# The second layer of the last 24 tiles in seven products instead of eight, and q and k turned by DMA

## The chip, the cores and the metric

The kernel runs on one core of a Trainium2 chip. The metric is the device time of one execution in microseconds (us); lower is better. The core has five engines that run side by side and wait for one another by semaphores: PE (TensorE, matmuls; PEld is its loading of weights), DVE (VectorE), ACT (ScalarE), POOL (GpSimd) and SP (SyncE, which here only issues DMAs). Each engine takes its instructions in the order in which they were written.

## The reference

Block-local attention, then a two-layer network on its output. Cut to what matters:

```python
# q, k, v: (8, 8, 576, 64) fp32: batch, heads, tokens, d; nine chunks of 64 tokens
scores = scale * np.matmul(q_c, k_c.transpose(0, 1, 2, 4, 3))   # within a chunk, 64 x 64
scores = scores - np.max(scores, axis=-1, keepdims=True)
attn = np.exp(scores)
attn = attn / (np.sum(attn, axis=-1, keepdims=True) + 1e-09)
out = np.matmul(attn, v_c)
x = out.transpose(0, 2, 1, 3).reshape(4608, 512)
h = x @ w_in                      # 512 x 2048
g = np.maximum(0.01 * h, h)
return g @ w_out                  # 2048 x 512, fp32 result
```

## The kernel before, in words

All matmuls are in fp16 with fp32 sums. The 4608 tokens are 36 tiles (units) of 128 tokens, two chunks of 64 each. The program is one straight list: for every unit an attention round, and between the stages of a round pieces of the two layers for tokens whose attention is done.

**A round** `it` of the main loop (lines 455 to 488) does, in this order: scores of unit it-1 on PE (`stage_s`, Sp, L308, eight matmuls of 64 columns), their maximum and subtraction on DVE (`stage_m`, mx, L317; `stage_b`, sh, L321), exp on ACT (`stage_x`, ex, L327), sums, reciprocal and product on DVE (`stage_z`, z, ze, zi, L333 to L337; `stage_n`, en, L342), the turned probabilities et, for units from 9 on by a DMA transpose that SP issues (`stage_d`, L361), and for unit it-3 the values (`stage_v`, xp, L372) and their copy by ACT into xT (`stage_a`, L385). `fill(n)` between the stages takes n pieces of the layers from a fixed list; 2 + 2 + 2 in rounds to 16, then 2 + 2 + 3.

**q and k.** Scores need q and k with d on the partitions. Units to 8 load whole rows (`load_qk`) and turn them on PE (qp, kp). From unit 9 on, `load_qk_batch` (L86) loads q_d and k_d by 16 DMAs a batch in an order in which DVE's 32x32 block transposes complete the turn: `stage_dq` (L290) twice a round into QZ, which holds q between zeros so that two heads share a matmul, and `stage_dk` (L298) once into KT. These loads, v and the weights are issued by POOL, which casts fp32 to fp16 on the way.

**The layers.** A block is 128, 256 or 512 tokens. First layer (`mm1`, L155): weights w_inT stationary, the block's xT moving, four matmuls a 128-row slice of d_ff; ACT writes the leaky result to gT (`act1`, L170). Second layer (`mm2`, L180): gT stationary, w_outT moving, 16 matmuls of 512 columns a tile of 128 tokens; ACT copies oP to osb (`store`, L191) and SP stores it (L193). One piece is four matmuls of 512 columns or as many columns in narrower ones. The list holds block after block: all of a block's first layer, then all of its second. The last tile is cut in three parts of columns (`last`, L206, L216, L214, L217) so that the last store is small. The start is a list written out by hand (FRONT).

PSUM has four buffers for hT and oP, one each for qp, kp, Sp, and one for tpe and xp.

Of the kernel before, what the change touches and what calls it, by code (L numbers as in the profile page):

```python
# [16 lines left out]
def kernel(  # L17
# [27 lines left out]
    BLOCKS = [128] * 6 + [256] + [128] * 2 + [256] * 5 + [512] * 4  # L45
# [10 lines left out]
    xT = sbp.tile([128, NT, n_tok], FP16, name="xT")  # L56
# [17 lines left out]

    qkd: dict[int, tuple[bass.AP, bass.AP]] = {}

    def load_qk_batch(b):
        both = []
        for name, src in (("q_d", q), ("k_d", k)):
            t = sbp.tile([128, 2, 2, S // 32, 32], FP16, name=name, tag=name, bufs=2)  # L80
            for m in range(2):
                for s in range(2):
                    for dh in range(2):
                        p0 = s * 64 + dh * 32
                        h0 = 4 * m + 2 * s
                        nc.gpsimd.dma_start(  # L86
                            out=t[p0:p0 + 32, m, :, :, :].rearrange("p h b d -> p (h b) d"),
                            in_=src[b, h0:h0 + 2, :, dh * 32:dh * 32 + 32].rearrange("h (b t) d -> t (h b) d", t=32),
                        )
            both.append(t.rearrange("p m h b d -> p (m h) (b d)"))  # L90
        qkd[b] = tuple(both)
# [28 lines left out]
    for eng, name, src in ((nc.sync, "q_f", q), (nc.scalar, "k_f", k)):  # L120
        t = sbp.tile([128, H, D], FP32, name=name)
        eng.dma_start(out=t, in_=src[0, :, 0:G, :].rearrange("h p d -> p h d"))
        first.append(t)
# [8 lines left out]
        "g1 v0 g2 Q0 Q1 g3 Q2 Q3 g4 P0 P1 P2 P3 g5 v1 g6 g7 g8 D2 "  # L132
    )
    LOADERS = {"g": load_qk, "v": load_v, "Q": load_w_in_quarter, "P": load_w_out_quarter, "D": load_qk_batch}
# [6 lines left out]
    gT: dict[int, bass.AP] = {}  # L141
    oP: dict[tuple[int, int], bass.AP] = {}
    START = [sum(BLOCKS[:j]) for j in range(len(BLOCKS))]

    HT: dict[tuple[int, int], bass.AP] = {}
    parts: dict[tuple[int, int], int] = {}

    def mm1(j, a):
        tb, r0 = BLOCKS[j], START[j]
        nf = 512 // tb  # L150
        hT = psp.tile([128, nf, tb], FP32, name="hT", tag="mm", bufs=4)
        for i in range(nf):
            fc = nf * a + i
            for t in range(NT):
                nc.tensor.matmul(  # L155
                    out=hT[:, i, :],
                    lhsT=w_inT[:, t, fc * 128:(fc + 1) * 128],
                    rhs=xT[:, t, r0:r0 + tb],
                    start=(t == 0),
                    stop=(t == NT - 1),  # L160
                )
        HT[j, a] = hT

    def act1(j, a):
        tb = BLOCKS[j]
        nf = 512 // tb
        if j not in gT:
            tag, bufs, pad = ("gS", 4, 128) if tb == 128 else ("gT", 2, 512)
            gT[j] = sbp.tile([128, NFC, tb], FP16, name="gT", tag=tag, bufs=bufs, padded_shape=[128, NFC, pad])
        nc.scalar.activation(  # L170
            out=gT[j][:, nf * a:nf * a + nf, :], in_=HT.pop((j, a)), func=AFT.Prelu, bias=0.0, scale=1.0, alpha=0.01
        )

    def mm2(j, ti, part):
        n = parts.get((j, ti), 0)
        if n == 0:
            oP[j, ti] = psp.tile([128, d_model], FP32, name="oP", tag="mm", bufs=4)
        o = oP[j, ti]
        for fc in range(part * 4, part * 4 + 4):
            nc.tensor.matmul(  # L180
                out=o,
                lhsT=gT[j][:, fc, ti * 128:(ti + 1) * 128],
                rhs=w_outT[:, fc, :],
                start=(n == 0 and fc == part * 4),
                stop=(n == NFC // 4 - 1 and fc == part * 4 + 3),
            )
        parts[j, ti] = n + 1

    def store(j, ti):
        osb = sbp.tile([128, d_model], FP32, name="osb", tag="osb", bufs=3)  # L190
        nc.scalar.activation(out=osb, in_=oP.pop((j, ti)), func=AFT.Copy, bias=0.0, scale=1.0)  # L191
        r0 = START[j] + ti * 128
        nc.sync.dma_start(out=out[r0:r0 + 128, :], in_=osb)  # L193

    def last(j, ti):
        r0 = START[j] + ti * 128
        osb = sbp.tile([128, d_model], FP32, name="osb", tag="osb", bufs=3)
        for c0, c1, copy, queue in (
            (0, d_model // 2, nc.scalar, nc.sync),
            (d_model // 2, 3 * d_model // 4, nc.scalar, nc.scalar),  # L200
            (3 * d_model // 4, d_model, nc.vector, nc.sync),
        ):
            part = slice(c0, c1)
            o = psp.tile([128, d_model], FP32, name="oP", tag="mm", bufs=4)
            for fc in range(NFC):
                nc.tensor.matmul(  # L206
                    out=o[:, :c1 - c0],
                    lhsT=gT[j][:, fc, ti * 128:(ti + 1) * 128],
                    rhs=w_outT[:, fc, part],
                    start=(fc == 0),  # L210
                    stop=(fc == NFC - 1),
                )
            if copy is nc.vector:
                copy.tensor_copy(out=osb[:, part], in_=o[:, :c1 - c0])  # L214
            else:
                copy.activation(out=osb[:, part], in_=o[:, :c1 - c0], func=AFT.Copy, bias=0.0, scale=1.0)  # L216
            queue.dma_start(out=out[r0:r0 + 128, part], in_=osb[:, part])  # L217

    def c1(j):
        return [("mm1", j, a, 0) for a in range(NFC * BLOCKS[j] // 512)]  # L220
# [3 lines left out]

    chunks = []
    for j in range(len(BLOCKS)):
        chunks += c1(j) + c2(j)
    state = {"tokens": 0}

    def fill(n):  # L230
        for _ in range(n):
            if not chunks:
                return
            kind, j, a, p = chunks[0]
            if START[j] + BLOCKS[j] > state["tokens"]:
                return
            chunks.pop(0)
            if kind == "mm1":
                mm1(j, a)
                act1(j, a)  # L240
            elif j == len(BLOCKS) - 1 and a == BLOCKS[j] // 128 - 1:
                if p == 0:
                    last(j, a)
# [4 lines left out]

# [29 lines left out]
    def stage_k(u):  # L278
        KT[u] = sbp.tile([128, 4, 2, CH], FP16, name="KT", tag="KT", bufs=3)
        nc.scalar.activation(out=KT[u], in_=KP.pop(u), func=AFT.Copy, bias=0.0, scale=1.0)  # L280

    def cuts(u):
        r0, r1 = u * G, (u + 1) * G
        cut = min(-(-r0 // S) * S, r1) if r0 % S else r1
        return [(a // S, a % S, (a - r0) // CH, (z - a) // CH) for a, z in ((r0, cut), (cut, r1)) if a < z]

    def stage_dq(u, s):
        qz = QZ[u % NQZ]
        for b, at, e0, n in cuts(u):
            nc.vector.transpose(  # L290
                out=qz[s * CH:(s + 1) * CH, :, e0:e0 + n, s, :],
                in_=qkd[b][0][s * CH:(s + 1) * CH, :, at:at + n * CH].rearrange("p h (e t) -> p h e t", e=n),
            )

    def stage_dk(u):
        KT[u] = sbp.tile([128, 4, 2, CH], FP16, name="KT", tag="KT", bufs=3)
        for b, at, e0, n in cuts(u):
            nc.vector.transpose(  # L298
                out=KT[u][:, :, e0:e0 + n, :],
                in_=qkd[b][1][:, :, at:at + n * CH].rearrange("p h (e t) -> p h e t", e=n),  # L300
            )

    def stage_s(u):
# [7 lines left out]
        SP[u] = Sp  # L311

    MX: dict[int, bass.AP] = {}

    def stage_m(u):
        MX[u] = sbp.tile([128, 8], FP32, name="mx", tag="mx", bufs=2)
        nc.vector.tensor_reduce(out=MX[u], in_=SP[u], axis=AXL.X, op=ALU.max)  # L317

    def stage_b(u):
# [3 lines left out]
        )  # L323

    def stage_x(u):
        E[u] = sbp.tile([128, 8, CH], FP16, name="ex", tag="ex", bufs=2)
        nc.scalar.activation(out=E[u], in_=SH.pop(u), func=AFT.Exp, bias=0.0, scale=SCL)  # L327

    ZI: dict[int, bass.AP] = {}

    def stage_z(u):
# [5 lines left out]
        nc.vector.reciprocal(out=ZI[u], in_=ze)  # L337

    def stage_n(u):
# [4 lines left out]
        )  # L344

    def stage_e(u):
# [4 lines left out]
        TP[u] = tpe  # L351

    def stage_c(u):
# [3 lines left out]
        ET[u] = et  # L357

    def stage_d(u):
# [4 lines left out]
        ET[u] = et  # L364

    def stage_v(u):
        et = ET.pop(u)
        xp = psp.tile([128, NT, 2, CH], FP32, name="xp", tag="ox", bufs=1)
        for e in range(2):
            b, c = divmod(2 * u + e, NCH)  # L370
            for t in range(NT):
# [3 lines left out]
                    rhs=et[:, t // 2, e, t % 2, :] if u < UD else et[:, t % 2, e, t // 2, :],  # L375
# [3 lines left out]
            if c == NCH - 1 and b + NVB < B:  # L379
                load_v(b + NVB)  # L380
        XP[u] = xp

    def stage_a(u):
        xp = XP.pop(u)
        nc.scalar.activation(out=xT[:, :, u * G:(u + 1) * G], in_=xp, func=AFT.Copy, bias=0.0, scale=1.0)  # L385
        state["tokens"] = (u + 1) * G


    def idle(n):
        t = psp.tile([128, 4, 128], FP32, name="idle", tag="mm", bufs=4)  # L390
# [3 lines left out]
    def first_layer(j, a):  # L394
        chunks.remove(("mm1", j, a, 0))
        mm1(j, a)

    def second_layer(j, p):
        chunks.remove(("mm2", j, 0, p))
        mm2(j, 0, p)  # L400
# [53 lines left out]

    for it in range(6, NU + 3):
        dve = UD <= it < NU
# [4 lines left out]
        if dve:  # L461
            stage_dq(it, 0)
# [6 lines left out]
        if dve:  # L469
            stage_dq(it, 1)  # L470
            stage_dk(it)
        elif it < UD:
# [4 lines left out]
            stage_k(it)  # L477
        if it <= NU:
# [41 lines left out]
```

## Time and profile before

| What | Value |
|---|---|
| median of 3 runs | 294.21 us (294.01 to 294.56) |
| profiled execution, span from first to last instruction | 292.1 us (no other time of it is given) |
| PE busy | 283.5 us, 2564 matmuls |
| DVE busy | 183.8 us, 343 instructions |
| ACT busy | 155.2 us, 268 instructions |
| POOL busy | 119.5 us, 148 instructions |
| hT, L155, 1152 matmuls | 135.1 us |
| oP, L180, 560 matmuls | 128.6 us |
| QZ, L290, 60 transposes | 38.2 us |
| KT, L298, 30 transposes | 19.4 us |

The busy time of an engine is the union of its instructions. A group's mean is the length of one instruction with its latency, so for pipelined matmuls it is longer than the distance from one start to the next. A wait line names who waited, for whom, the total, the number of times and the longest. A timeline line gives start, length, engine, line, operation, output <- inputs, count, and in brackets the idle time before it with what ended it.

### The profile page before, as it was taken

The page shows a single profiled execution, that of the slowest core. Times are in us where ns is not written, and L with a number is a line of the kernel's source. Part 1 is how long each engine was busy: PE and PEld are TensorE (multiplying, and loading weights), DVE is VectorE, ACT ScalarE, POOL GpSimd, SP SyncE. Part 2 cuts the span into 40 slices and gives each one's busy share as a digit, 9 for nine tenths or more (in the row PEclk, how much of TensorE's full clock was granted, in tenths as well). Part 3 has the DMA queues.
Part 4 walks back from the last instruction along what each step waited for, and adds up shares of the span by engine and source line. Part 5 has one row for each costly group of instructions (what it writes and reads, how often), then busy time and mean ns, then how long its engine had stood idle before and what let it go on. Part 6 is the DMA issues. An engine that isn't in the chain of part 4 may idle for free.

```text
span 292.1 us, 6233 instructions
## 1 busy us (share of the span) xinstructions
PE 283.5 (97%) x2564; PEld 181.0 (62%) x2564; DVE 183.8 (63%) x343; ACT 155.2 (53%) x268; POOL 119.5 (41%) x148
## 2 busy tenths in 40 slices
PE   4989999999999999999999999999999999999995
PEld 4979845888677766767676744444445444444444
DVE  6987417789899998777787788778876730000000
ACT  6457623666555555646564647734873377127511
POOL 8867547998408936913295369130000000000000
PEclk9999999999999999999999999999999999999999
DMA  9999999999969999999499399999111320120022
GB/s 132 169 193 193 203 157 198 151 148 144 124 97 96 162 78 158 154 142 90 101 107 132 61 159 147 78 65 163 54 20 54 73 91 0 38 81 28 0 74 72
DMA packets 192476, 32.00 MB, mean 110 GB/s; under 512 B 183488, under 2 KB 187968, under 8 KB 192448
## 3 DMA queue, kind: packets, MB, share of 16 engines
q0 software_dynamic: 170208, 18.10, 117.7%
q1 hardware_dynamic: 21056, 13.18, 18.1%
q10 hardware_dynamic: 1184, 0.33, 0.5%
q8 instruction: 20, 0.33, 0.5%
q14 instruction: 8, 0.07, 0.1%
HBM read 36.70 MB, written 9.44 MB: 158 GB/s over the span
## 4 chain that ended last, share of the span: by engine, by line
PE 93%; DVE 3%; DMA 2%; ACT 1%; issue 1%; DVEq 0%
PE hT L155 43%; PE oP L180 41%; PE xp L372 3%; PE Sp L308 3%; DMA k_f<-in_k_dram 2%; PE oP L206 1%; PE tpe L350 1%; PE kp L268 1%; DVE mx L317 0%; DVE z L333 0%; DVE sh L321 0%; DVE en L342 0%; PE qp L263 0%; ACT ex L327 0%; DVE VB L420 0%
## 5 line engine op out<-in xcount | busy, mean ns | idle before, releaser
L155 PE MATMUL hT<-xT,w_inT 128*128 128x128 f16 (+2 forms) x1152 | 135.1, 272 | 0.2 <-issue 0.2
L180 PE MATMUL oP<-w_outT,gT 128*128 128x512 f16 x560 | 128.6, 379 | 0.0
L155 PEld LDWEIGHTS <-w_inT 128*128 128x128 f16 x1152 | 90.0, 98 | 33.4 <-issue 0.5
L170 ACT ACTIVATE gT<-hT 128x512 f16<-128x512 f32 x144 | 85.7, 596 | 34.8 <-PE hT L155 33.0
L180 PEld LDWEIGHTS <-gT 128*128 128x128 f16 x560 | 52.5, 98 | 55.8
L191 ACT ACTIVATE osb<-oP 128x512 f32<-128x512 f32 x35 | 20.9, 597 | 61.3 <-PE oP L180 58.7
L86 POOL DMA_DIRECT2D q_d<-in_q_dram x48 | 38.7, 821 | 32.0 <-DVE QZ L290 28.0
L317 DVE TENSOR_REDUCE mx<-Sp 128x8 f32<-128x512 f32 x36 | 24.9, 691 | 32.6 <-PE Sp L308 32.5
L86 POOL DMA_DIRECT2D k_d<-in_k_dram x48 | 38.7, 824 | 0.9 <-issue 0.5
L290 DVE STREAM_TRANSPOSE QZ<-q_d 64x512 f16<-64x512 f16 (+1 forms) x60 | 38.2, 644 | 0.4
L214 DVE COPY osb<-oP 128x128 f32<-128x128 f32 x1 | 0.3, 290 | 51.4 <-PE oP L206 51.4
L327 ACT ACTIVATE ex<-sh 128x512 f16<-128x512 f32 x36 | 22.5, 626 | 15.0 <-DVE sh L321 14.8
L385 ACT ACTIVATE xT<-xp 128x512 f16<-128x512 f32 x36 | 21.4, 594 | 16.4 <-PE xp L372 16.3
L95 POOL DMA_DIRECT2D VB<-in_v_dram x16 | 18.5, 1162 | 28.0 <-PE xp L372 28.0
L333 DVE TENSOR_REDUCE z<-ex 128x8 f32<-128x512 f16 x36 | 23.6, 654 | 3.9 <-ACT ex L327 3.8
L342 DVE TENSOR_TENSOR en<-ex,zi 128x512 f16<-128x512 f16 x36 | 24.9, 691 | 1.4 <-DVE zi L337 0.2
L321 DVE TENSOR_TENSOR sh<-Sp,mx 128x512 f32<-128x512 f32 x36 | 24.9, 691 | 1.2
L298 DVE STREAM_TRANSPOSE KT<-k_d 128x512 f16<-128x512 f16 (+1 forms) x30 | 19.4, 654 | 0.8
L372 PEld LDWEIGHTS <-VB 128*128 128x128 f16 x288 | 13.1, 98 | 6.8 <-issue 1.2
L308 PEld LDWEIGHTS <-QZ 128*128 128x128 f16 x288 | 13.2, 99 | 5.4 <-issue 0.3
L372 PE MATMUL xp<-et,VB 128*128 128x64 f16 x288 | 14.3, 193 | 1.1 <-DVE et L356 1.1
L308 PE MATMUL Sp<-KT,QZ 128*128 128x64 f16 x288 | 14.5, 194 | 0.2 <-ACT KT L280 0.2
(37 smaller groups left out, 112.2 us busy)
## 6 DMA issues: line engine op xcount, KB each, us to landing
out_dram<-osb SPq DMA_DIRECT2D x35, 256.0 KB, 2.3
VB<-in_v_dram POOLq DMA_DIRECT2D x16, 288.0 KB, 6.5
q_d<-in_q_dram POOLq DMA_DIRECT2D x48, 72.0 KB, 5.3
k_d<-in_k_dram POOLq DMA_DIRECT2D x48, 72.0 KB, 5.2
w_inT<-in_moe_w_in_dram POOLq DMA_DIRECT2D x8, 256.0 KB, 8.8
w_outT<-in_moe_w_out_dram POOLq DMA_DIRECT2D x4, 512.0 KB, 9.5
q_in<-in_q_dram POOLq DMA_DIRECT2D x7, 128.0 KB, 9.3
k_in<-in_k_dram POOLq DMA_DIRECT2D x7, 128.0 KB, 9.3
```

The costliest lines, as they stand in the source:

```text
L86: nc.gpsimd.dma_start(out=t[p0:p0 + 32, m, :, :, :].rearrange("p h b d -> p (h b) d"), in_=src[b, h0:h0 + 2, :, dh * 32:dh * 32 + 32].rear ...
L155: nc.tensor.matmul(out=hT[:, i, :], lhsT=w_inT[:, t, fc * 128:(fc + 1) * 128], rhs=xT[:, t, r0:r0 + tb], start=(t == 0), stop=(t == NT - 1),)
L170: nc.scalar.activation(out=gT[j][:, nf * a:nf * a + nf, :], in_=HT.pop((j, a)), func=AFT.Prelu, bias=0.0, scale=1.0, alpha=0.01)
L180: nc.tensor.matmul(out=o, lhsT=gT[j][:, fc, ti * 128:(ti + 1) * 128], rhs=w_outT[:, fc, :], start=(n == 0 and fc == part * 4), stop=(n == ...
L290: nc.vector.transpose(out=qz[s * CH:(s + 1) * CH, :, e0:e0 + n, s, :], in_=qkd[b][0][s * CH:(s + 1) * CH, :, at:at + n * CH].rearrange("p ...
L308: nc.tensor.matmul(out=Sp[:, i, :], lhsT=qz[:, 2 * m + g, e, :, :], rhs=kt[:, 2 * m + g, e, :], start=True, stop=True)
L317: nc.vector.tensor_reduce(out=MX[u], in_=SP[u], axis=AXL.X, op=ALU.max)
L321: nc.vector.tensor_tensor(out=SH[u], in0=SP.pop(u), in1=MX.pop(u).unsqueeze(2).to_broadcast((128, 8, CH)), op=ALU.subtract)
L327: nc.scalar.activation(out=E[u], in_=SH.pop(u), func=AFT.Exp, bias=0.0, scale=SCL)
L333: nc.vector.tensor_reduce(out=z, in_=E[u], axis=AXL.X, op=ALU.add)
L342: nc.vector.tensor_tensor(out=E[u], in0=ex, in1=ZI.pop(u).unsqueeze(2).to_broadcast((128, 8, CH)), op=ALU.mult)
L372: nc.tensor.matmul(out=xp[:, t, e, :], lhsT=VB[b % NVB][:, t, c, :], rhs=et[:, t // 2, e, t % 2, :] if u < UD else et[:, t % 2, e, t // 2, :],
```

## The change

**Seven products.** The last 24 tiles become six blocks of 512 tokens. The second layer of such a block, a 512 x 2048 matrix g times w_out (2048 x 512), is cut into 2 x 2 quarters on both sides, and Strassen's scheme forms the four quarters of the result from seven products m1 to m7 of sums of quarters instead of eight products of quarters. Five sums of quarters of w_out (WF) are made once by DVE, in rounds 11 to 15; five sums of quarters of gT (S1, S2, S5, S6, S7) by DVE for each block. Each product is 2 x 8 matmuls of 256 columns into one of three PSUM banks (a, b, c: the buffers of qp and kp and one of the four of hT and oP). m4 adds onto m2's bank, m5 onto m3's, m6 onto m1's, m7 onto m4's. ACT copies out m3, m4, m5 (td, osb), DVE combines the rest (td, tw, tt, osb), and each half of a block, 256 tokens, is stored by one DMA of 512 KB. The last tile's narrow parts are gone.

**q and k.** `load_qk` for all units, six rounds ahead; from unit 9 on, two DMA transposes on SP (`stage_t`, two rounds ahead, in front of et's) turn q and k into QT and KT, and POOL copies QT between the zeros of QZ in two copies of 64x512 (`stage_p`). DVE's block transposes are gone. The next load of v is issued by POOL at the end of a round instead of in its middle.

**Order.** Blocks before the 24 tiles are 6 x 128 and 3 x 256. Products of a block are merged with the first layer of the next one. While the program is built, times are kept for PE, DVE and ACT (T), and `fill` takes the first piece of each kind whose inputs are ready by these times, else the one that is ready earliest. Pieces a round: 6, in rounds 12 to 19 five.

```diff
-    BLOCKS = [128] * 6 + [256] + [128] * 2 + [256] * 5 + [512] * 4
+    BLOCKS = [128] * 6 + [256] * 3 + [512] * 6
+    PLAIN = 9
+    SUB = {7: 128}
+    RING = 1536
+    HB, HM = NFC // 2, d_model // 2
...
+    def weight_form(i):
+        of, by, op = WFORMS[i]
+        nc.vector.tensor_tensor(out=WF[:, i], in0=of, in1=by, op=op)
+        on("dve", 1.24)
...
+        a11, a12 = g[:, :HB, :n], g[:, HB:, :n]
+        a21, a22 = g[:, :HB, n:2 * n], g[:, HB:, n:2 * n]
+        of, by, op, to = {
+            "S2": (a21, a22, ALU.add, None),
+            "S1": (a11, a22, ALU.add, None),
+            "S5": (a11, a12, ALU.add, None),
+            "S6": (a21, a11, ALU.subtract, a21),
+            "S7": (a12, a22, ALU.subtract, a12),
+        }[name]
...
+        nc.vector.tensor_tensor(out=to, in0=of, in1=by, op=op)
+    FORMS = ("S2", "S1", "S5", "S6", "S7")
...
+        for fc in range(HB):
+            nc.tensor.matmul(
+                out=BANK[bank][:, p, :],
+                lhsT=lhs[:, fc, p * 128:(p + 1) * 128],
+                rhs=rhs[:, fc, :],
+                start=(opens and p == 0 and fc == 0),
+                stop=(fc == HB - 1),
...
+        if m == 2:
+            nc.vector.tensor_tensor(out=TMP["d"], in0=TMP["d"], in1=BANK["b"], op=ALU.subtract)
+        elif m == 1:
+            nc.vector.tensor_tensor(out=temp("w", j), in0=BANK["c"], in1=TMP["d"], op=ALU.add)
+        elif m == 5:
+            nc.vector.tensor_tensor(out=temp("t", j), in0=TMP["w"], in1=osb_of(j, 0)[:, :, HM:], op=ALU.subtract)
+        elif m == 6:
+            nc.vector.tensor_tensor(out=osb_of(j, 1)[:, :, HM:], in0=BANK["c"], in1=TMP["d"], op=ALU.add)
+            store_side(j, 1)
+        elif m == 7:
+            nc.vector.tensor_tensor(out=osb_of(j, 0)[:, :, :HM], in0=BANK["b"], in1=TMP["t"], op=ALU.add)
+            store_side(j, 0)
...
+    ORDER = (3, 2, 1, 4, 5, 6, 7)
...
-    def stage_dq(u, s):
-        qz = QZ[u % NQZ]
-        for b, at, e0, n in cuts(u):
-            nc.vector.transpose(
...
+    def stage_t(u):
+        for i, (name, to) in enumerate((("QT", QT), ("KT", KT))):
+            to[u] = sbp.tile([128, 4, 2, CH], FP16, name=name, tag=name, bufs=(3, 6)[i])
+            nc.sync.dma_start_transpose(
+                out=to[u].rearrange("p i e t -> p i (e t)"), in_=qk[u][i].rearrange("p h d -> p (h d)")
+            )
+    def stage_p(u):
+        qt = QT.pop(u)
+        for s in range(2):
+            part = slice(s * CH, (s + 1) * CH)
+            nc.gpsimd.tensor_copy(out=QZ[u % NQZ][part, :, :, s, :], in_=qt[part])
...
+    ROUND = [0] * 6 + [6] * 6 + [5] * 8 + [6] * 8 + [6] * 11
     for it in range(6, NU + 3):
-        dve = UD <= it < NU
         if it <= NU:
             stage_s(it - 1)
             stage_m(it - 1)
             stage_b(it - 1)
-        if dve:
-            stage_dq(it, 0)
         fill(2)
...
+        if UD <= it < NU:
+            stage_p(it)
+        if UD <= it + 2 < NU:
+            stage_t(it + 2)
...
+        if 11 <= it < 16:
+            weight_form(it - 11)
         if it <= NU:
             stage_z(it - 1)
             stage_n(it - 1)
             if it - 1 >= UD:
                 stage_d(it - 1)
         fill(2)
+        due = free_v[:]
         values(it - 2 if it - 2 < UD else it - 3 if it - 3 >= UD else -1)
-        fill(3 if dve and it >= 17 else 2)
-        for b in range(3, B):
-            if it == 9 * b // 2 - 4:
-                load_qk_batch(b)
+        fill(ROUND[it] - 4)
+        for b in due:
+            load_v(b)
+            free_v.remove(b)
+        if UD + 3 <= it + 6 < NU:
+            load_qk(it + 6)
```

More of the change, by code (lines that the diff above doesn't have):

```diff
@@ L186, in mm2 @@
             )
+        on("pe", UNIT)
         parts[j, ti] = n + 1
     def store(j, ti):
-        osb = sbp.tile([128, d_model], FP32, name="osb", tag="osb", bufs=3)
+        osb = sbp.tile([128, d_model], FP32, name="osb", tag="osb", bufs=3, padded_shape=[128, 2 * d_model])
         nc.scalar.activation(out=osb, in_=oP.pop((j, ti)), func=AFT.Copy, bias=0.0, scale=1.0)
+        on("act", 0.62, T["pe"] + 0.2)
         r0 = START[j] + ti * 128
         nc.sync.dma_start(out=out[r0:r0 + 128, :], in_=osb)
[L195 to L217, printed above, removed]
@@ L225, with after, forms @@
     chunks = []
-    for j in range(len(BLOCKS)):
+    for j in range(PLAIN):
         chunks += c1(j) + c2(j)
+    chunks = [x for j in range(PLAIN) for x in c1(j) + c2(j)] + c1(PLAIN)
+    for j in range(PLAIN, len(BLOCKS)):
+        chunks += merged(c7(j), c1(j + 1), 1.5) if j + 1 < len(BLOCKS) else c7(j)
     state = {"tokens": 0}
+    later: list[list] = []
+    def after(n, what):
+        later.append([n, what])
+    sums: list[tuple[int, str]] = []
+    def forms(n, slack=1.0):
+        while n and sums and T["dve"] <= T["pe"] + slack:
+            j, name = sums[0]
+            if when["gT", j] > T["pe"] + slack:
+                return
+            if name in ("S2", "S1", "S5") and j > PLAIN and (j - 1, int(name[1])) not in done:
+                return
+            sums.pop(0)
+            form(j, name)
+            n -= 1
@@ new lines, with ready @@
+    LEFT: dict[int, int] = {}
+    for x in chunks:
+        LEFT[x[1]] = LEFT.get(x[1], 0) + 1
+    def ready(x):
+        kind, j, a, p = x
+        if kind == "mm1":
+            end = START[j] + (p + 1) * sub(j)
+            if end > state["tokens"] or any(LEFT[i] for i in range(j) if tile_of(i) == tile_of(j) - 2):
+                return None
+            return when["x", end]
+        if made.get(j, 0) < NFC * BLOCKS[j] // 512:
+            return None
+        if kind == "mm2":
+            return when["gT", j]
+        needs = [("gT", j), BANKS[a] + (j if a > 3 else j - 1,)]
+        if a not in (3, 4):
+            needs.append((f"S{a}", j))
+        at = 0.0
+        for y in needs:
+            t = when.get(y, 0.0 if y[-1] < PLAIN else None)
+            if t is None:
+                return None
+            at = max(at, t)
+        return at
@@ new lines, with pick @@
+    BANKS = {3: ("evict", 5), 2: ("combine", 7), 1: ("combine", 6), 4: ("combine", 2), 5: ("evict", 3), 6: ("combine", 1), 7: ("evict", 4)}
+    def pick():
+        first: dict[str, tuple] = {}
+        for x in chunks:
+            first.setdefault(x[0], x)
+        can = [(ready(x), x) for x in chunks if first[x[0]] == x]
+        can = [(t, x) for t, x in can if t is not None]
+        if not can:
+            return None
+        if any(0 < n < NFC // 4 for n in parts.values()):
+            can = [(t, x) for t, x in can if x[0] == "mm2"]
+        return next((x for t, x in can if t <= T["pe"]), min(can, key=lambda y: y[0])[1])
@@ L230, in fill, with follow @@
+    def follow():
+        for y in later:
+            y[0] -= 1
+        while any(y[0] < 0 for y in later):
+            y = next(y for y in later if y[0] < 0)
+            later.remove(y)
+            y[1]()
     def fill(n):
         for _ in range(n):
-            if not chunks:
+            x = pick()
+            while x is None and (later or sums):
+                if later:
+                    later.pop(0)[1]()
+                else:
+                    form(*sums.pop(0))
+                x = pick()
+            if x is None:
@@ L233, in fill @@
                 return
[L234 to L237, printed above, removed]
+            T["pe"] = max(T["pe"], ready(x))
+            chunks.remove(x)
+            kind, j, a, p = x
+            LEFT[j] -= 1
             if kind == "mm1":
[L239 to L243, printed above, removed]
+                mm1(j, a, p)
+                act1(j, a, p)
+                if j >= PLAIN and made[j] == NFC * BLOCKS[j] // 512:
+                    sums.extend((j, name) for name in FORMS)
+            elif kind == "m":
+                product(j, a, p)
+                if p == BLOCKS[j] // 256 - 1:
+                    evict(j, a)
+                    if a in (1, 2, 5, 6, 7):
+                        after(1, lambda j=j, a=a: combine(j, a))
@@ L247, in fill @@
                     store(j, a)
+            follow()
+            forms(1)
+            if not chunks:
+                while later:
+                    later.pop(0)[1]()
     QP: dict[int, bass.AP] = {}
```

218 lines of the change are left out of this document (160 added, 58 removed).

## The prediction

> **What bounds the kernel now.** I read the busy shares and the slices first, then what PE waited for, then one stretch of PE and of DVE instruction by instruction, then the groups, the DMAs and the end.
>
> ```profile
> span 292.1 us, 6233 instructions
> PE 283.5 (97%) x2564; PEld 181.0 (62%) x2564; DVE 183.8 (63%) x343; ACT 155.2 (53%) x268; POOL 119.5 (41%) x148
> PE   4989999999999999999999999999999999999995
> ...
> PEclk9999999999999999999999999999999999999999
> ```
>
> PE is full in every slice but the first, the third and the last, at full granted clock. The waits of PE alone:
>
> ```profile
> PE idle L392 <- POOL ident masks.py:199: 3.8, 1, 3.8
> PE xp L372 <- DVE et L356: 1.1, 1, 1.1
> PE hT L155 <- issue: 0.2, 1, 0.2
> PE Sp L308 <- ACT KT L280: 0.2, 1, 0.2
> ```
>
> 5.3 us in all, all in the start. So the time is PE's work plus the two ends, and a PE matmul removed is time removed as long as PE stays fed. What a matmul costs is read from start to start, because ends are modelled (start, length, engine, line):
>
> ```profile
> 121.74 3.62 PE L180 MATMUL oP<-w_outT,gT 128*128 128x512 f16 x16
> 125.19 0.40 PE L372 MATMUL xp<-et,VB 128*128 128x64 f16 x8
> 125.43 2.75 PE L180 MATMUL oP<-w_outT,gT 128*128 128x512 f16 x12
> 128.02 0.40 PE L308 MATMUL Sp<-KT,QZ 128*128 128x64 f16 x8
> 128.25 3.66 PE L155 MATMUL hT<-xT,w_inT 128*128 128x256 f16 x32
> 131.74 0.40 PE L372 MATMUL xp<-et,VB 128*128 128x64 f16 x8
> ```
>
> 512 columns take (125.19-121.74)/16 = 216 ns, 256 columns (131.74-128.25)/32 = 109 ns, eight of 64 columns 0.23 us. Half the columns cost half, new weights each time. A piece of work (four of 512, or eight of 256) is 0.86 to 0.87 us. From 121.51, the Sp before these lines, to the Sp at 128.02 a round of one attention unit takes 6.51 us: seven pieces and 0.46.
>
> **PE's part.** Second layer of the last 24 tiles: now 23 x 16 x 216 ns = 79.4, plus the last tile's narrow parts (line 206, 3.55 us on the chain) = 83.0 us. After: 6 blocks x 7 products x 2 x 8 = 672 matmuls of 256 columns x 109 ns = 73.3. In the first layer 256 matmuls of 256 columns (27.9) become 128 of 512 (27.6). PE loses 9.7 + 0.3 = **10.0 us**. Everything else below is what is given back.
>
> **DVE's part.** Rounds get shorter: 6 pieces and 0.46 = 5.7 us, in rounds 12 to 19 five pieces, 4.8 us. Rows for DVE:
>
> ```profile
> 129.18 0.69 DVE L321 TENSOR_TENSOR sh<-Sp,mx 128x512 f32<-128x512 f32 x1
> 129.78 1.42 DVE L290 STREAM_TRANSPOSE QZ<-q_d 64x512 f16<-64x512 f16 x2
> 131.23 0.71 DVE L298 STREAM_TRANSPOSE KT<-k_d 128x512 f16<-128x512 f16 x1
> 131.87 0.64 DVE L333 TENSOR_REDUCE z<-ex 128x8 f32<-128x512 f16 x1
> ...
> 132.99 0.69 DVE L342 TENSOR_TENSOR en<-ex,zi 128x512 f16<-128x512 f16 x1
> ```
>
> Removed: the three transposes, 2.1 us a round, 57.6 in all (groups of lines 290 and 298). They stood in the shadow of ACT's ex (0.62 us, some 0.85 with its signals). What stays is mx to the end of sh, 1.42, and z to the end of en, 1.81: 3.23 a round.
> Added: 35 sums of 128x2048 16-bit elements (five for the weights, five for each block) and 30 combinations of 128x512 fp32, like sh, 0.69. No row shows a sum of 2048. The fixed part of a DVE instruction comes from QZ's transposes, 701 ns for 512 elements and 416 for 256: 131 ns. The copy et (16-bit in and out) takes 424 ns for 512, so 0.57 ns an element and **1.30 us** for 2048; en (one fp32 operand) takes 691, which makes 2.37. I take 1.30, the row whose operands are all 16-bit, and keep 2.37 as an end. [...]
>
> A block of products fills five rounds (14 pieces and the next block's 16): 28.4 us of PE. DVE there: 5 x 3.23 + 5 x 1.30 + 5 x 0.69 = 26.1, plus ex's shadow where the order of the built kernel puts nothing into it (two rounds of 0.85) or only a combination (two of 0.15): **28.1 of 28.4**. DVE is as full as PE in these 15 rounds. In the second round of a block m2's combination (td) comes after S5, the softmax and en, some 6.0 us into the round, and m4 takes its bank at 6.6: 0.6 us of room. I put 1.0 us for lateness there, between nothing and the rival below. The weight sums stand in ex's shadow in rounds 11 to 15: 1.42 + 1.30 + 1.81 = 4.5 of 4.8, so nothing; uncovered they would cost 6.5.
>
> Two places have no first-layer work to put between products. (a) Block 9, the first: S2 needs ACT's last gT piece and 1.30 us, 2.15 after that piece's matmuls (0.2 signal, 0.60 evict, 1.30, signals), while PE has 1.97 of work; S1 stands behind mx and sh, done at 4.95, where mb ends at 4.0. **1.3 us**. (b) Block 14, the last: S2 0.5 late as ma takes 1.75; then td stands behind S1, S5 and S6 and ends at 6.75, so m4 waits from 5.75 to 6.85. **1.6 us**.
>
> **The end.** Now the last piece is small:
>
> ```profile
> 288.94 0.29 DVE L214 COPY osb<-oP 128x128 f32<-128x128 f32 x1 [51.36 <-PE oP L206]
> 289.26 0.33 SPq L217 DMA_DIRECT2D out_dram<-osb  x1
> ```
>
> From this copy's start to landing 1.9 us (landing 1.6 for 64 KB). After: a combination, 0.69, and a store of 512 KB. Landings in the quiet end are 1.6, 1.7, 2.0 us for 64, 128, 256 KB; doubling once more gives 2.6 (3.5 by the busy median of 2.3). 0.69 + 0.1 + 2.6 = 3.4 to 4.3: **1.6 us** more, at most 2.4.
>
> **SP, POOL, DMA.** SP gets two transposes of q and k a round beside et's, ahead of en's wait:
>
> ```profile
> L361 SPq DMA_TRANSPOSE et<-en x27: 1189/1196/2182, 74.6 to 237.7; - x27
> DMA to landing us min/median/max: 2.4/4.4/6.5
> ```
>
> Three at 1.2 and a store at 0.33 to 1.0: 4.0 to 4.6 of 4.8. Behind a waiting et stand the stores (ACT waits for osb, three buffers) and the next round's two. et is issued 4.5 us into its round and needed 13.4 after that round's start (two rounds and 3.7), so some 4.5 us of room at the median landing. Cost nothing; if that cover goes, see the rivals.
> POOL in the eight short rounds: 8 x (0.875 + 0.844) for q_in and k_in, 1.7 for one tile cut in two, 4 x 1.16 for v, and 16 copies of 64x512. No row shows one; memset and affine select of 128 elements take 243 and 287 ns, 98 for one element, so 0.68 to 0.86 us for 512 (1.15 with no fixed part). With 0.86, 33.9 of 38.4 us; with 1.15 it is just full. Each copy is needed a round after its input is there. Nothing. The small packets of q_d and k_d (96 x 1152) give way to half as many; DMA gets lighter.
>
> **Sum.** 292.1 - 10.0 + 1.3 + 1.6 + 1.6 + 1.0 = 287.6 for the span. No time but the span is given for the profiled execution; the runs' median is 294.21, so 2.1 us lie around it. **289.7 us**, 1.5% faster. 0.2% (0.6 us) is about what a measurement of this kernel can tell from no change.
>
> **Rivals.**
> 1. POOL's copies hold DVE up (slower). Place: the 15 rounds with products, where DVE has 0.06 us to spare a round. Price: one copy of 0.68 to 0.86 lost a round gives 15 x 0.62 to 0.80 = 9.3 to 12.0 in place of the 1.0, time 298 to 301, I take 299. It decides from (4.5 + 1.0)/15 + 0.06 = 0.43 us a round. For it: DVE has no room, and sums, en and the copies all read SBUF. Against: beside 119 us of POOL's work en took 691 to 694 ns in all 36 cases; but that POOL work is DMA issue, no copy. [...] 0.20, of this 0.02 within 0.2%.
> 2. The sums run at en's rate, 2.37 us: 5.3 us more DVE a block, 15 us in three blocks, some 2 more in (a) and 4 in (b): about 310. 0.07.
> 3. SP: transposes right behind one another take the 1.98 us seen once in the quiet part (231.64). 1.2 + 2 x 1.98 + 0.57 = 5.7: 0.9 over in eight short rounds, 7.2, less 4.5 of room: 2.7 more, 292.4. 0.09, of this 0.03 within 0.2%.
> 4. DVE has the time and PE never waits: only the end's 1.6 is given back, 283.7 + 2.1 = 285.8. 0.12.
> Forecast 0.52. That products are not what they claim can't be: 672 matmuls of 256 columns stand in the built order.
>
> Faster 0.52 + 0.12 + 0.06 = 0.70, within 0.05, slower 0.18 + 0.07 = 0.25. The range runs from rival 4 to just under rival 1's price, 285.8 to 298.5; it leaves out rival 2 and about half of rival 1, some 0.17.
>
> **What would show it.** PE busy near 274; its waits named td, S2, S1 or m4 at the two places, 3 us, and little in rounds 12 to 19. The sums' mean: 1.2 to 1.3 or 2.4. POOL's copies and en's largest duration: above 0.7 means held up. SP's transposes: 1.2 or 2. The last store's landing. Wrong if PE's waits grow past 10 us spread over the rounds, whoever is named.

## The result and the profile after

| What | Before | After |
|---|---|---|
| median | 294.3 us (294.01 to 294.56) | **291.05 us** (290.44 to 291.99) |
| ratio to before | | 0.9896, 95% interval 0.9875 to 0.9917 |
| profiled execution | span 292.1 us | 290.96 us, span 289.2 us |
| end of PE's last matmul, and the tail behind it | 288.86, 3.2 us | 284.39, 4.8 us |

The change is worth 3.2 us, 1.0%. The forecast was 289.7. PE lost the 10 us that it was to lose; 7.1 us were given back, not the 5.5 of the sum. Medians, here and below, are over all executions of a kernel, and ratios leave out those over 1.5% above its fastest. First the page of the changed kernel, its span and busy times:

```profile
span 289.2 us, 6592 instructions
PE 275.5 (95%) x2692; PEld 194.4 (67%) x2692; DVE 192.2 (66%) x317; ACT 151.7 (52%) x261; POOL 129.1 (45%) x166
```

PE is busy 8 us less with a span 2.9 us shorter: it now has holes. Here is what PE waited for (who, for whom, us in total, times, longest):

```profile
PE idle L635 <- POOL ident masks.py:199: 3.8, 1, 3.8
PE xp L611 <- DMA et<-en: 1.8, 4, 0.7
PE xp L611 <- DVE et L592: 0.9, 1, 0.9
PE mc L293 <- DVE S L263: 0.5, 1, 0.5
PE hT L171 <- issue: 0.5, 1, 0.5
PE mb L293 <- DVE td L329: 0.3, 1, 0.3
PE xp L611 <- DMA VB<-in_v_dram: 0.3, 1, 0.3
PE mb L293 <- DVE S L263: 0.2, 1, 0.2
```

The first, third and fifth line belong to the start (before had the same kinds, 5.3 us in all). The waits for S and td at the two transitions were forecast, and are smaller than forecast. The largest new one was not: xp, four times, for the turned probabilities et. Since the ends of matmuls are modelled, a wait line understates what is lost. From start to start, the six xp groups held up for et (at 98.73, 114.04, 119.18, 130.31, 171.40 and 205.64 us) lose 0.13 + 0.86 + 0.34 + 0.68 + 0.52 + 0.17 = 2.7 us, and the one held for v (206.24) 0.47.

One of them in the timeline (start, length, engine, line):

```profile
99.85 0.40 PE L537 MATMUL Sp<-KT,QZ 128*128 128x64 f16 x8
104.34 0.69 DVE L576 TENSOR_TENSOR en<-ex,zi 128x512 f16<-128x512 f16 x1
104.48 1.27 SPq L521 DMA_TRANSPOSE KT<-k_in  x1
105.85 1.21 SPq L598 DMA_TRANSPOSE et<-en  x1
...
114.04 0.41 PE L611 MATMUL xp<-et,VB 128*128 128x64 f16 x8 [0.71 <-DMA et<-en]
```

The round starts with Sp at 99.85. en is done at 105.03, 5.2 us into it; SP is still at k's transpose and comes to et at 105.85, 6.0 into it; the two matmuls in front of xp start at 112.74 and take 0.22 us each, so it would have started at 113.2, 13.3 into it (the prediction had 13.4). It starts when et has landed, 8.2 us after its issue.

Why et lands late shows in the DMA engines' view of the main stretch, 90 to 200 us (busy tenths in 40 slices, then the queues with packets, MB and the time of their packets, then et's median landing). Before:

```profile
DMA  9999991999999970992399999940999999980699
q0 software_dynamic: 93254, 7.08, 168.7%
et<-en SPq DMA_TRANSPOSE x18, 4.9
```

After:

```profile
DMA  9999999999999999999999999999989999999999
q0 software_dynamic: 53009, 6.69, 101.8%
et<-en SPq DMA_TRANSPOSE x20, 8.1
```

There are fewer packets in the stretch, 86498 against 104475 over all queues, but more bytes (17.79 MB against 13.06), and no hole left: before, ten of the 40 slices are below nine tenths, three of them at 0; after, one, at 8.

### The profile page after: what moved, and what is told of

The parts are those of the page before. It is cut to its first block, busy times and chain, and to the rows that moved or that the text cites. A ratio compares the mean times of both kernels' runs of the same rounds, so it can differ in the third digit from the quotient of the medians.

```text
span 289.2 us, 6592 instructions
## 1 busy us (share of the span) xinstructions
PE 275.5 (95%) x2692; PEld 194.4 (67%) x2692; DVE 192.2 (66%) x317; ACT 151.7 (52%) x261; POOL 129.1 (45%) x166
## 3 DMA queue, kind: packets, MB, share of 16 engines
q0 software_dynamic: 114336, 18.09, 88.2%
q1 hardware_dynamic: 50096, 20.33, 41.7%
## 4 chain that ended last, share of the span: by engine, by line
PE 54%; DMA 35%; POOL 5%; DVE 2%; issue 1%; ACT 1%; SPq 0%; POOLq 0%
PE hT L171 25%; DMA VB<-in_v_dram 14%; PE oP L203 12%; DMA q_in<-in_q_dram 12%; PE mb L293 5%; PE ma L293 4%; PE mc L293 4%; DMA w_inT<-in_moe_w_in_dram 3%; DMA QT<-q_in 3%; DMA et<-en 3%; PE xp L611 1%; PE Sp L537 1%; POOL VB L82 1%; DVE S L263 1%; POOL w_inT L89 1%
## 5 line engine op out<-in xcount | busy, mean ns | idle before, releaser
L171 PE MATMUL hT<-xT,w_inT 128*128 128x128 f16 (+2 forms) x1024 | 142.4, 286 | 0.6 <-issue 0.5
L171 PEld LDWEIGHTS <-w_inT 128*128 128x128 f16 x1024 | 76.3, 98 | 31.2 <-issue 1.0
L530 POOL COPY QZ<-QT 64x512 f16<-64x512 f16 x54 | 37.6, 696 | 44.3 <-DMA QT<-q_in 39.0
L293 PEld LDWEIGHTS <-gT 128*128 128x128 f16 x384 | 37.5, 98 | 13.4 <-issue 0.5
L203 PE MATMUL oP<-w_outT,gT 128*128 128x512 f16 x192 | 44.7, 379 | 0.0
L73 POOL DMA_DIRECT2D k_in<-in_k_dram x39 | 33.1, 849 | 16.6 <-DMA k_in<-in_k_dram 6.2
L73 POOL DMA_DIRECT2D q_in<-in_q_dram x39 | 33.1, 851 | 10.4 <-DMA VB<-in_v_dram 4.4
L566 DVE TENSOR_REDUCE z<-ex 128x8 f32<-128x512 f16 x36 | 24.6, 684 | 18.6 <-ACT ex L559 18.5
L293 PEld LDWEIGHTS <-S 128*128 128x128 f16 x288 | 27.9, 98 | 10.3 <-DVE S L263 1.5
L559 ACT ACTIVATE ex<-sh 128x512 f16<-128x512 f32 x36 | 22.6, 627 | 14.2 <-DVE sh L552 14.1
L263 DVE TENSOR_TENSOR S<-gT 128x2048 f16<-128x2048 f16 x18 | 22.6, 1283 | 4.1 <-ACT gT L191 4.1
L293 PE MATMUL mb<-WF,gT 128*128 128x256 f16 x192 | 24.6, 273 | 0.3 <-DVE td L329 0.3
L215 ACT ACTIVATE osb<-oP 128x512 f32<-128x512 f32 x12 | 7.2, 597 | 16.5 <-PE oP L203 16.5
## 6 DMA issues: line engine op xcount, KB each, us to landing
VB<-in_v_dram POOLq DMA_DIRECT2D x16, 288.0 KB, 14.1
q_in<-in_q_dram POOLq DMA_DIRECT2D x31, 128.0 KB, 12.2
```

What stands on the lines that cost most here:

```text
L73: nc.gpsimd.dma_start(out=t[a - r0:z - r0], in_=src[a // S, :, a % S:a % S + z - a, :].rearrange("h p d -> p h d"),)
L171: nc.tensor.matmul(out=hT[:, i, :], lhsT=w_inT[:, t, fc * 128:(fc + 1) * 128], rhs=xT[:, t, r0 % RING:r0 % RING + tb], start=(t == 0), sto ...
L203: nc.tensor.matmul(out=o, lhsT=gT[j][:, fc, ti * 128:(ti + 1) * 128], rhs=w_outT[:, fc, :], start=(n == 0 and fc == part * 4), stop=(n == ...
L263: nc.vector.tensor_tensor(out=to, in0=of, in1=by, op=op)
L293: nc.tensor.matmul(out=BANK[bank][:, p, :], lhsT=lhs[:, fc, p * 128:(p + 1) * 128], rhs=rhs[:, fc, :], start=(opens and p == 0 and fc == 0 ...
L530: nc.gpsimd.tensor_copy(out=QZ[u % NQZ][part, :, :, s, :], in_=qt[part])
```

## The experiments

Each ratio is to the kernel before, with its 95% interval. The changed kernel's own ratio is 0.9896.

### E1 and E2: is it the order in SP's queue?

```diff
# E1: the same two lines, moved behind stage_d; E2: and one round earlier, with four QT
-        if UD <= it + 2 < NU:
-            stage_t(it + 2)
...
             if it - 1 >= UD:
                 stage_d(it - 1)
+        if UD <= it + 2 < NU:
+            stage_t(it + 2)
```

> Only the order on SP: et's transpose of a round is issued ahead of the two that turn q and k, still two rounds ahead. My theory (queue): PE's 2.7 us of waits for et come from et standing behind the other two transposes on SP; the waits for et go below 0.5 us, but QT lands 1.3 us later, has about 1 us of room, and Sp begins to wait for POOL's copies: 290 to 291.5 us. Rival (engines): POOL's load packets share the DMA engines, landing stays at 7 us or more whatever the order, et gains only its 1.1 us of earlier issue, waits for et halve, 290 us.

Measured: 292.77 us, 0.9947 (0.9921 to 0.9974). The waits for et are gone (its median landing over the whole run goes from 7.4 to 5.8 us, where the other theory had it stay at 7 or more), but Sp waits 3.9 us for KT and 1.9 for QZ, twice each.

> As the run before, and q and k are turned three rounds ahead instead of two (QT in four buffers). Queue theory: no wait for et and none for Sp, 2.7 to 3.2 us less than the changed kernel, 288 us. Engines rival: landing of et stays at 7 us or more, half of the waits stay, 289.7 us.

Measured: 291.88 us, 0.991 (0.9887 to 0.9933). KT and QZ are in time, and et is late again: 3.3 us in PE's row, landing 7.6. The order only chooses which transfer is late. The theory of the queue's order falls; and E2 did not gain what the other theory had allowed it either.

### E3 and E4: take part of either traffic away

E3 takes away one of the three transposes of a round (and gives QT six buffers, since its tile then serves as KT too), E4 one of the two loads of q and k.

```diff
# E3
-        for i, (name, to) in enumerate((("QT", QT), ("KT", KT))):
+        for i, (name, to) in enumerate((("QT", QT),)):
...
+            to[u] = sbp.tile([128, 4, 2, CH], FP16, name=name, tag=name, bufs=6)
...
+        KT[u] = QT[u]
# E4, in load_qk
+            if u >= UD + 3 and name == "k_in":
+                both.append(both[0])
+                continue
```

> Leaves out the transposes of k from unit 9 on; the scores are computed with q's turned tile in k's place. Two transposes a round instead of three, loads unchanged. Queue theory: et's landing falls from 7.4 us to under 5, PE's waits for et vanish, 288 us. Engines rival: landing falls to 6 us at most, waits fall by a third, 290 us.

> Leaves out the loads of k from unit 12 on; q's tile is turned twice and serves as k. Three transposes a round as before, POOL's load packets nearly halved. Queue theory: et's landing stays above 6.5 us and the waits for et stay near 2.7 us, 290.5 to 291 us. Engines rival: landing falls to under 5 us, the waits vanish, 288 us.

Measured: E3 287.6 us, 0.9777 (0.9762 to 0.9791); E4 287.61 us, 0.9775 (0.9758 to 0.9792). Neither has a wait for et, for v or for a q or k turned by DMA in PE's rows, and over the whole run et lands in 4.1 and 4.0 us. The same view of 90 to 200 us for E4:

```profile
DMA  9969999999999999998962499997996699978843
et<-en SPq DMA_TRANSPOSE x21, 4.1
```

The holes are back: 13 slices below nine tenths (8 in E3). This is the run that tells the theories apart: E4 leaves every transpose on SP where it was, so SP's time to issue them is not the limit; E3 leaves every load of POOL's, so the loads alone are not either. Nor did q and k come too late for SP: in SP's rows of the changed kernel no transpose of q or k waits for its load. Two loads a round, two transposes a round and et's together fill the DMA engines (one of the 40 slices below nine tenths), and either of them taken away frees 3.4 us, about what the late et and VB (2.7 + 0.5) cost by the starts. et's transposes are issued by SP and the loads by POOL: E4, which takes away loads alone, brings et's landing to 4.0 us from 7.4, so in this kernel transfers issued by one engine hold up those issued by another.

### E5 and E6: the two halves alone

E5 keeps the turning by DMA and does all second layers plainly, in eight products. E6 keeps the seven products and turns q and k on DVE as before.

```diff
# E5
-    PLAIN = 9
+    PLAIN = 15
...
-        if 11 <= it < 16:
-            weight_form(it - 11)
...
# E6, beside the loads by batch and stage_dq(it, 0) as before
-            stage_p(it)
-        if UD <= it + 2 < NU:
-            stage_t(it + 2)
+            stage_dq(it, 1)
+            stage_dk(it)
```

> Undoes the products and keeps the rest: the last six blocks' second layer is 16 matmuls of 512 columns a tile again, no sums, no weight forms; q and k still turned by DMA, same pieces a round (the xT ring is larger so that it fits). My theory (PE bound, DMA full in the attention rounds): PE's work rises by 9.7 us; the two transitions (0.7 and 0.85) and the late store (about 1) go; waits for et of about 3 us stay: 291.05 + 9.7 - 2.6 = 298 us, slower than the kernel before, since the turn by DMA costs and brings PE nothing. Rival (the products or the sums on DVE cost more than the trace shows): under 296 us.

Measured: 297.95 us, 1.011 (1.0085 to 1.0136), as expected. So the seven products are worth 297.95 - 291.05 = 6.9 us net, and the turning by DMA with the new order costs 297.95 - 294.3 = 3.7 by itself. The terms of the trace say about the same: 10.0 less 0.83, 0.86 and 1.6 (the transitions and the end) is 6.7, and 2.7 + 0.5 + 0.6 (et, VB and two places before 60 us, named further down) is 3.8.

> Undoes the q and k part and keeps the products: q_d and k_d loaded and turned by DVE's block transposes as before, one DMA transpose a round. My theory (DVE has no room in the rounds with products): DVE gets 2.1 us more a round, about 8 us more than PE in a block of five rounds, 24 us in three blocks, and 0.6 us a round in the eight short ones: 310 to 320 us, PE's waits at products and Sp. Rival (DVE's work is off the path, only the DMAs matter): DMA is freed of two transposes a round, 288 to 291 us.

Measured: 319.11 us, 1.0845 (1.0817 to 1.0872). In these rounds the products can't do without the turning by DMA: DVE is busy 241.6 us, and PE waits for it:

```profile
PE mc L311 <- DVE gT L281: 6.6, 2, 4.6
PE Sp L578 <- DVE KT L567: 5.9, 7, 1.4
PE mb L311 <- DVE gT L281: 5.2, 1, 5.2
```

The time was in the expected range, but not all for the expected reason. Behind the 5.2 us of idleness, which ended at 211.9, the view by stretches has (busy times; the granted clock is the third number from the end):

```profile
211.90:215.40 3.50, 3.45 (x23) 2.59 (x24) 2.27 (x2) 0.60 (x1) 0.00 (x0) 0.50 0.44 159
```

Half clock. There are four such stretches, 6.8 + 3.4 + 6.8 + 3.4 = 20.4 us. In part of them PE was waiting anyway; from start to start, the matmuls that ran at half rate cost 7.8 us of the 319. No theory had them.

### E7: POOL's copies left out

```diff
-            stage_p(it)
```

> Leaves out POOL's copies of q between the zeros: from unit 9 on the scores use the q that was there before. Everything else stays. Theory (POOL's copies shut DVE out now and then but DVE's lateness is not on the path): en falls to 691 ns in all cases, S to 1.22 us, the time stays within 0.7 us of 291. Rival (the copies hold DVE up and DVE holds PE): 2 us or more faster, 289 or less, with the waits for et gone.

Measured: 291.75 us, 0.9935 (0.9905 to 0.9964), no faster. But DVE is rid of something. Of the groups of DVE from 60 to 205 us (mean ns after the busy time), the changed kernel has

```profile
L576 DVE TENSOR_TENSOR en<-ex,zi 128x512 f16<-128x512 f16 x26 | 19.0, 732 | 0.9
L263 DVE TENSOR_TENSOR S<-gT 128x2048 f16<-128x2048 f16 x9 | 12.1, 1346 | 1.9 <-ACT gT L191 1.9
```

and E7

```profile
L577 DVE TENSOR_TENSOR en<-ex,zi 128x512 f16<-128x512 f16 x26 | 18.0, 692 | 0.9
L263 DVE TENSOR_TENSOR S<-gT 128x2048 f16<-128x2048 f16 x9 | 11.0, 1219 | 1.8 <-ACT gT L191 1.8
```

With the copies, en takes 691 to 1102 ns; without, 691 to 694 in all 36. That is rival 1's mechanism, and it is shown. Its price is not there: DVE's busy time falls by 192.2 - 187.8 = 4.4 us over 27 rounds with copies, 0.16 a round, below the 0.43 from which it was to decide.

### E8 and E11: more work a round, more loads a round

E8 gives the rounds 6 and 7 pieces instead of 5 and 6, so that et has more time; E11 loads k a second time, into a tile that nobody reads.

```diff
# E8
-    ROUND = [0] * 6 + [6] * 6 + [5] * 8 + [6] * 8 + [6] * 11
+    ROUND = [0] * 6 + [6] * 6 + [6] * 8 + [7] * 8 + [7] * 11
# E11, in load_qk
+        if u >= UD + 3:
+            extra = sbp.tile([128, H, D], FP16, name="extra", tag="extra", bufs=2)
...
+            nc.gpsimd.dma_start(
...
```

> Only the pieces a round: 6 instead of 5 in rounds 12 to 19 and 7 instead of 6 after that, so a round is 0.87 us longer and the attention ends later; loads and transposes stay the same in number. Theory (the DMA engines are full per round): et's landing falls below 6 us and the waits for et vanish (3 us), but PE runs out of first-layer work, products of blocks 9 to 12 come unmixed as in block 14 and wait for their sums, 0.5 to 1 us a block: 289.5 to 291.5 us. Rival (et is late for a reason that does not depend on the length of a round): waits for et stay at 2 to 3 us and the sums come on top, 293 us or more.

Measured: 297.9 us, 1.0137 (1.0117 to 1.0157), a miss. The waits for et did go (0.4 left), though et's landing hardly moved (6.9 us; the theory had it below 6): a longer round gives it more room. But hT now waits 5.2 us, three times, for ACT's xT: with seven pieces the first layer runs out of tokens whose attention is done. I had not priced that. The products' waits for S and td grow too, from 1.0 to 3.8 us.

> Adds work: from unit 12 on each tile of k is loaded a second time into a buffer that nobody reads (in units cut in two, the first part only); 128 KB more a round on POOL's queue. Theory (the DMA engines are full per round, each load moved costs or gives its share): leaving a load out gave 3.4 us, which was all the waits there were; one more load a round has no such floor, et and QT come later every round, PE's waits for et, KT and QZ grow by 5 us or more: 296 to 305 us. Rival (there is room, and leaving a load out helped for another reason): within 1 us of 291.

Measured: 309.57 us, 1.0513 (1.0492 to 1.0533): slower, by more than the theory's range, but not on its path. PE's rows have no wait for et, and et lands in 7.1 us, no later than the changed kernel's 7.4. Sp waits 13.8 us for QZ, four times, up to 6.0. Ahead of the longest of these waits, which ended at 143.0, POOL stood at two load issues until earlier loads had landed, and the copies into QZ stood behind them in its queue:

```profile
134.71 0.87 POOL L73 DMA_DIRECT2D k_in<-in_k_dram  x1 [3.61 <-DMA VB<-in_v_dram]
140.74 0.87 POOL L83 DMA_DIRECT2D extra<-in_k_dram  x1 [5.16 <-DMA extra<-in_k_dram]
141.66 1.28 POOL L539 COPY QZ<-QT 64x512 f16<-64x512 f16 x2
```

The extra tile has two buffers, and POOL stood 13.2 us, four times, for earlier loads into it. So E11 shows that a third load a round has no room in POOL's queue as it is built here; that more traffic makes et later it does not show. Half clock follows for 3.4 + 3.4 + 6.8 = 13.6 us; the matmuls at half rate in it cost 6.0 of the 18.5 us.

### E9, E12 and E13: the end and the first transition

E9 forms td ahead of S6 in the last block and cuts the last stores, so that the last one is 128 KB. E13 also makes S1 right behind S2 in block 9, ahead of mx and sh. E12 is E13 with v's load issued in the round in which its buffer comes free, instead of one round later.

```diff
# all three
...
+            if name == "S6" and j == len(BLOCKS) - 1 and ("combine", 2, j) not in when:
+                return
...
+        nc.vector.tensor_tensor(
+            out=osb_of(j, 0)[:, p, :HM], in0=BANK["b"][:, p, :], in1=TMP["t"][:, p, :], op=ALU.add
+        )
+        store_half(j, 0, 0, p, p + 1)
# E12 and E13
+            if j == PLAIN and name == "S2":
+                sums.pop(0)
+                form(j, "S1")
# E12
-        due = free_v[:]
...
-        for b in due:
+        for b in free_v[:]:
```

> Only the last block: td before S6 on DVE, and the last stores cut (left and right halves of columns as they come, m7 combined and stored a tile at a time, 128 KB last). Expected from the trace: m4 starts 0.49 us earlier, the last combination takes 0.42 instead of 0.69, the last landing 1.7 instead of 3.0 us: 2.0 us faster, 289.0 us. Rival: the end is set by the earlier store of 512 KB, at most 0.5 us.

Measured: 290.57 us, 0.9866 (0.984 to 0.9891), half a microsecond below the changed kernel by the medians, with intervals that overlap. The profiled execution, the fastest of its six, has a span of 287.5. In it m4 starts without a wait and the tail behind PE shrinks from 4.8 to 3.3 us, but 0.5 us is lost again: m7's second half writes to the bank whose first half DVE is reading, and waits for it.

```profile
283.19 1.03 PE L293 MATMUL mb<-WF,gT 128*128 128x256 f16 x8 [0.51 <-DVE osb L331]
```

> The tail of e9 together with two small moves: in block 9 S1 is made right behind S2, ahead of mx and sh, and v's next load is issued in the round in which its buffer comes free instead of one round later. Expected: 1.7 us from the tail, 0.5 to 0.6 at mc of block 9, 0.4 at the wait for VB: 288.4 us, 2.6 below the changed kernel. Rival: v's loads a round earlier crowd the transposes and et's waits grow by what the others save, 290.5 us.

Measured: 292.65 us, 0.9931 (0.9911 to 0.9952), a miss. Sp waits 4.1 us for QZ, twice, because the copies into QZ stand in POOL's queue behind loads that wait. Issued in the same round, v's load waits there until PE's xp has read the old buffer (13.1 us in POOL's rows, five times; 1.8, once, in the changed kernel). And the next load of q or k waits, by the profile, until v's has landed (22.3 us, eight times; 8.5, four times, in the changed kernel); the longest of Sp's waits, 3.2 us, follows one of these:

```profile
175.46 0.87 POOL L73 DMA_DIRECT2D k_in<-in_k_dram  x1 [6.32 <-DMA VB<-in_v_dram]
```

Why a load of k should wait for the landing of v's, the trace doesn't say. In this profiled execution 3.4 us at half clock follow Sp's longest wait, as they do in E1's, so only the waits of these two are read here, not their spans. The load's place one round later, which I had taken for a loss, costs less than the earlier one.

> The version with td ahead of S6 and the last stores cut, and in block 9 S1 made right behind S2, ahead of mx and sh; the loads of v stay where the changed kernel has them. Theory: the first product of block 9 waits 0.5 us for S1 in the changed kernel; with S1 there 0.7 us sooner that wait goes, while mx and sh have 5 us before anything on PE asks for them. So 0.5 us below the version with the tail alone (290.6): 290.0, and 1.0 below the changed kernel. Rival: the waits for et by DMA, which come out anew in each run, move the time by as much as that: 290.3 to 291.0, no difference from the version with the tail alone. The wait of mc for S of block 9 is gone from PE's rows in either case.

Measured: **289.9 us**, 0.9846 (0.9812 to 0.988), the fastest of those that leave nothing out. The wait of mc for S is gone. Its interval and E9's (0.984 to 0.9891) overlap for the most part, and it barely overlaps the changed kernel's 0.9875 to 0.9917: that it beats the kernel before is measured, that it beats the changed one by the 1.1 us between the medians is likely, and whether S1's place adds to E9 is not told. In its profile the waits for et and VB are 2.7 and 1.3 us, more than in the changed kernel's: this scatter is what hides half a microsecond.

## Why the prediction came out as it did

The direction and the bulk were right; the time was 1.35 us above the forecast. By its steps:

- **PE's 10.0 us: right.** PE's busy time falls by 8 us only, because ends are modelled and a part of every hole counts as busy. From start to start, this was given back: 0.4 in the start (the first oP matmul stands at 35.47 instead of 35.07 us), 0.2 in the first layer at 55.8 us, for which PE's rows name nothing, 0.83 and 0.86 at the transitions, 3.2 for et and VB, and 1.6 at the end. That is 7.1, and 292.1 - 10.0 + 7.1 = 289.2, the span. The 0.4 and the 0.2 were in no step.
- **The sums, 1.30 of 1.30 to 2.37: right.** In the quiet stretch from 212 us on their means are 1216 and 1220 ns. My 1.30, worked out from et's copy, was 0.08 too long. Rival 2 is out.
- **The two transitions, 1.3 + 1.6: the right places, a little over half the size.** Block 9 lost 0.83 (mb 0.13 and mc 0.70, both for S) and block 14 0.86 (mb 0.37 for S, m4 0.49 for td), part of it because each sum is shorter than I took it for. DVE's lateness, 1.0, shows nowhere in PE's rows.
- **The end, 1.6: right,** 1.6 measured; the last store lands in 2.8 us, of 2.6 to 3.5.
- **The step that failed is "SP, POOL, DMA", where it says "Cost nothing" and "DMA gets lighter".** It cost 3.2 us at PE. The sum had et issued 4.5 us into its round, 4.4 of landing, needed at 13.4: 4.5 of room. In the round shown above it is issued at 6.0 (0.7 for DVE's en, 0.8 for SP's transposes in front) and lands in 8.2, at 14.2, where it was needed at 13.3: 0.9 too late. Most of the loss of room is the landing, and I had kept the landing of the kernel before. I had counted packets; they did get fewer, and the packets' time falls from 117.7 + 18.1% to 88.2 + 41.7% of the span. But those shares add up packets in flight beside one another (168.7% for one queue above), so they don't say how full the engines are. The slices do, and before only ten of 40 were below nine tenths.
- **Rival 1: the mechanism is real, the price a quarter.** What would show it, en above 0.7 us, is there (up to 1102 ns, sums up to 1628). E7 confirms it: with no copies en stays at 691 to 694. sh and mx, which take Sp from PSUM, have 693 and 692 as their longest even with the copies. But a copy meets en or a sum only now and then (en is above 0.7 us in 6 of 36 cases); "one copy lost a round" was too much, and between the two transitions none of PE's waits names DVE.
- **Rival 3: its place was right, not its mechanism.** The transposes of q and k take 1.3 and 1.4 us on SP in the median and up to 3.05, so SP had little room in the short rounds. But E4, with the same transposes on SP, has no wait.

Errors of both signs met: the DMA cost 3.2 us and the two places before 60 us 0.6 that the sum had at nothing, while the transitions and DVE's lateness cost 2.2 less than it had. So the near hit is in part luck and says little for the sum.

What stays open is what inside the DMA engines is used up, the number of small packets, the bytes, or turning itself. E3 and E4 take away 14,700 and 25,000 packets of different kinds, 3.6 and 3.2 MB, with the same effect, and the trace doesn't say which packet held up which.

## What to carry to other kernels

Before moving work from an engine to DMA, look at the slices of the DMA engines in the stretch concerned, not at packets or at queue shares: where they show few holes, as here, a landing time of the kernel before can't be carried over (et's went from 4.4 to 7.4 us), and a transfer with "room" must be priced at the landing of a full system (8.1 from 90 to 200 us). When a load is late, take part of the traffic away, of either kind, before another order is tried: here that freed 3.4 us, and the order only chose which tile was late. And take POOL's copies beside DVE's sums and products as a small tax (0.16 us of DVE a round here) that matters only where DVE is on the path.

## What the runs showed of the hardware that was not expected

- The granted clock fell in the middle of E1, E6, E11 and E12, for 3.4 or 6.8 us at a time. E6's is 1.00 in the first 2.4 us of its wait of 5.2 and 0.50 from then on, 3.9 us of it with PE at work again, and eight matmuls of 256 columns take 1.69 us from start to start where they took 0.87. From start to start, waits of 2.2 us in E6 and 2.7 in E1 brought half clock, and waits of 2.6 in E8 and 2.0 in E13 did not, so the length of the wait alone does not tell it. E6's two waits of about 5 us cost 7 to 8 each in all.
- A copy of 64x512 16-bit elements on POOL takes 602 to 614 ns in 43 of 54 cases (bounds were 680 to 860) and up to 1496 when it meets DVE's en or a sum (the longest stood beside a sum of the weights that took 1511 ns, where the other four take 1.21 or 1.22 us): both sides pay.
- Landings moved far under the same bytes: v's 288 KB went from 6.5 to 14.1 us, with fewer packets in all, and q's 128 KB take 12.2 in the changed kernel and 7.5 where k's loads are left out (E4).
